# Building the convolution kernels: rounding by TensorE inside PSUM, a written-out order for the first two units, and a new layout of the staging tiles

## The chip, the cores and the metric

The program runs on one core of one Trainium2 chip. The metric is the device time of one execution in microseconds (us), taken as the median over runs. A core has five engines that work at the same time, each through its own queue of instructions in order: TensorE (PE in the profile; its weight loads are listed apart as PEld), VectorE (DVE), ScalarE (ACT), GpSimd (POOL) and SyncE (SP), which here only issues DMAs. [...]

## What is computed

Four layers on a 2048 x 640 activation: a state-space convolution, an attention with one shared key and value head, and both once more. The change lies in what both convolutions need first, the convolution kernel of each of the 640 channels d at 2048 times l:

```python
dt = exp(log_dt)[:, None]
logdA = dt * (A_re + 1j * A_im)                 # 640 x 128 states n
dB = dt * (B_re + 1j * B_im)
P = exp(logdA[:, :, None] * l[None, None, :])
K = einsum("dn,dnl,dn->dl", C, P, dB).real      # 640 x 2048
```

K is the same in both convolution layers and is computed once, at the start of the program. The kernel splits l = 32 i + s, and so writes the exponential as a product of a factor for i (64 values) and a factor for s (32 values), each a magnitude exp(...) times a cosine and a sine of an angle. The sum over the 128 states is a matmul.

## The kernel before, in words

**Tables.** `kg_tables` (L203) makes, on VectorE and ScalarE, what the angles and magnitudes are built from: for each state and channel the angle per step in whole turns (`thr`), the angle of 32 steps (`th1`), the phase of C times B (`ph`), the decay (`are`) and a log magnitude (`lw`). Each is split into three bf16 parts, staged in the tiles `hs[...]` (first in their pool, before the inputs and the scratch tiles that `t3` makes), and sent by SP into three tables that matmuls can read: `tb` (48 rows: three parts of 16 channels), `ta` and `tm` (96 rows). `send` (L222) goes through DRAM: one DMA out, then three back. `send_late` (L230) writes the lower 48 rows of `ta` or `tm` for one eighth q of the channels, three DMAs each time; q = 0 to 7 are sent one after the other, the last after all else. The order of ScalarE, VectorE and SP is written out by hand here; SP's issues of the input x (`load_x`, L611, eight DMAs of 640 KB) are not part of that order, and a planner puts them among the others.

**Units.** `_kgen` (L310) then runs 20 units u, each 2 x 16 channels. For a unit there are two angles (h = 0 from `tb`, h = 1 from `ta`) and three magnitudes (k = 0, 1, 2 from `tm`). Each is a 128 x 1024 tile in PSUM, made by two bf16 matmuls of 512 columns: the table's 16 channels by 128 states are the weights, and a constant tile `kg` is what streams.

- `phase_first(u, h)` (L366): the two matmuls of an angle into `ph`. There is one such PSUM buffer (`bufs=1`), so the next angle waits for the last reader.
- `phase(u, h)` (L374): VectorE takes the whole turns off in two passes, `magic_round` (L191; adding and subtracting 1.5 x 2^23 rounds to a whole number, kept in `r`) and a subtraction (L381), which leaves the fraction `f` in SBUF.
- `trig(u, h)` (L383): ScalarE takes Abs of `f` into `fa` (L394), Sin of `f` (L395) and Sin of a quarter turn less `fa`, the cosine (L396).
- `sizes` and `exps` (L399, L408): the matmuls of a magnitude into `pe` (two buffers) and Exp by ScalarE.
- `products(u, k)` (L416): six passes of VectorE, two for each k.
- `sums(u, ds)` (L433): the fp32 matmuls, 128 rows by 32 columns of weights and 64 columns of stream, four side by side in the array, in eight steps d. `store` (L444) copies the sum to `kst` and every fourth unit sends it to DRAM.

The loop at L469 is a software pipeline with the order of PE, ScalarE and VectorE written by hand. In iteration u stand the magnitudes and the trig of unit u, the angles of u + 1, the products of u - 1 and the sums of u - 2. Even and odd iterations differ in where Exp and Sin stand, so that ScalarE changes its table once per unit. From u = 5 to 12 VectorE also has the layer norm's statistics of one part of x (`stats`, L618). After u = 20 the tables' pool is closed and GpSimd loads the weights of the Fourier matmuls; the rest of the program, two convolutions and two attentions, follows.

## Time and profile before

| | |
|---|---|
| median of 3 runs | 3025.67 us (3024.11 to 3025.82) |
| the profiled execution | 3025.52 us, its span 3023.7 us |
| PE busy over the span | 2797.2 us (93%) |
| ScalarE busy over the span | 2427.3 us (80%) |
| VectorE busy over the span | 1402.3 us (46%) |
| tables and units (the part that the change touches) | about the first 300 us |

The page has six parts. Part 1 gives the busy time of each engine; part 2 cuts the span into 40 slices of 75.6 us, each digit being the busy share in tenths; "PEclk" is the clock that TensorE was granted. Part 4 follows back what ended last, part 5 lists the costliest groups of instructions, and part 6 the DMAs. Other views of the same execution list instructions in order of time with what each waited for, who waited for whom in a stretch, and the busy time of each engine in stretches that one chooses. A share over the whole span says little here: the attention layers, where PE and ScalarE are at 90% and over, fill three quarters of it, and the units are a stage of their own with another limit.

### The profile page before, as it was taken

To read this page: it belongs to the slowest core of one execution; us is meant where nothing else is said; L and a number is where in the kernel's file an instruction comes from. 1 tells how busy PE (TensorE), PEld (TensorE's weight loads), DVE (VectorE), ACT (ScalarE), POOL (GpSimd) and SP (SyncE) were. 2 spreads that over 40 slices of the span, in tenths; PEclk is the share of its full clock that TensorE was granted. 3 is DMA by queue.
4 is the path that set the end of the run, shared out by engine and by line. 5 is a ranking of instruction groups with operands and counts; after the bars stand their busy time and mean duration, and the time that the engine had idled before them with its cause. 6 is when DMAs were issued, how large, how long until landed. Compare 5 with 4: busy or idle time off the path is not lost. (4 is left out here: it accounts for less than half of the span.)

```text
span 3023.7 us, 52365 instructions
## 1 busy us (share of the span) xinstructions
PE 2797.2 (93%) x21696; PEld 1284.0 (42%) x21696; DVE 1402.3 (46%) x1788; ACT 2427.3 (80%) x2910; POOL 45.1 (1%) x117
## 2 busy tenths in 40 slices
PE   2776989998999999999999899798999999999998
PEld 0333979775233323333232689673233333323333
DVE  7999899942123232322323499721222223222222
ACT  5888333444999999999999532438999999999997
POOL 0001000000000000000000000000000000000000
PEclk9855999999999999999999999899999999999999
DMA  6114531133200010000100211131100101110100
GB/s 145 33 22 112 186 143 56 46 115 111 80 22 25 22 27 21 26 25 22 25 22 20 113 56 42 58 131 56 27 24 23 43 22 26 39 28 21 43 19 23
DMA packets 109104, 158.82 MB, mean 53 GB/s; under 512 B 58948, under 2 KB 65092, under 8 KB 105236
## 3 DMA queue, kind: packets, MB, share of 16 engines
q1 hardware_dynamic: 102680, 137.70, 15.7%
q0 software_dynamic: 4208, 16.67, 1.5%
q8 instruction: 175, 2.87, 0.4%
q10 hardware_dynamic: 1968, 0.98, 0.1%
q14 instruction: 73, 0.60, 0.1%
HBM read 95.22 MB, written 48.04 MB: 47 GB/s over the span
## 5 line engine op out<-in xcount | busy, mean ns | idle before, releaser
L1158 ACT ACTIVATE pt<-scb 128x1024 f32<-128x1024 f32 x1024 | 942.2, 1116 | 7.5 <-DMA qpb<-mxd 4.5
L1158 ACT ACTIVATE pt<-scd 128x1024 f32<-128x1024 f32 x1024 | 942.2, 1117 | 7.0 <-PE scd L1154 5.4
L1168 PE MATMUL pod<-pt,vt 128*32 128x512 f32 x4096 | 547.1, 606 | 4.4 <-DVE on L1185 0.2
L1168 PE MATMUL pob<-pt,vt 128*32 128x512 f32 x4096 | 547.0, 606 | 4.4 <-DVE on L1185 0.3
L1154 PE MATMUL scb<-qpb,kt 62*128 62x512 f32 x2048 | 385.9, 451 | 6.2 <-DVEq L1103 5.8
L1154 PE MATMUL scd<-qpd,kt 62*128 62x512 f32 x2048 | 385.9, 451 | 5.6 <-PEq L1103 5.3
L1154 PEld LDWEIGHTS scb<-qpb,kt 62*128 62x128 f32 x2048 | 165.9, 185 | 402.1 <-ACT pt L1158 392.6
L1154 PEld LDWEIGHTS scd<-qpd,kt 62*128 62x128 f32 x2048 | 166.0, 185 | 401.7 <-ACT pt L1158 392.4
L1216 DVE TENSOR_TENSOR x<-pyd,x 128x320 f32<-128x320 f32 x146 | 71.8, 492 | 560.8 <-PE pyd L1228 560.8
L1216 DVE TENSOR_TENSOR x<-pyb,x 128x320 f32<-128x320 f32 x146 | 71.8, 492 | 547.6 <-PE pyb L1228 547.6
L1188 DVE RECIPROCAL rc<-rc 128x512 f32<-128x512 f32 x62 | 207.9, 3354 | 2.1
L1168 PEld LDWEIGHTS pob<-pt,vt 128*32 128x32 f32 x4096 | 80.6, 108 | 178.2 <-issue 160.2
L1168 PEld LDWEIGHTS pod<-pt,vt 128*32 128x32 f32 x4096 | 80.6, 108 | 178.0 <-issue 160.0
L601 PE MATMUL za<-xna,wf 128*128 128x256 f32 x512 | 113.0, 383 | 2.5 <-ACT xna L757 2.5
L601 PE MATMUL zc<-xnc,wf 128*128 128x256 f32 x512 | 111.5, 379 | 2.7 <-ACT xnc L757 2.7
L603 ACT ACTIVATE Aa<-za 128x1024 f32<-128x1024 f32 x16 | 16.4, 1023 | 118.5 <-PE za L601 117.3
L603 ACT ACTIVATE Ac<-zc 128x1024 f32<-128x1024 f32 x16 | 16.4, 1023 | 113.7 <-PE zc L601 113.7
L1228 PE MATMUL pyd<-wo,ot 128*32 128x320 f32 x1168 | 105.3, 432 | 0.0
L1228 PE MATMUL pyb<-wo,ot 128*32 128x320 f32 x1168 | 105.3, 432 | 0.0
L601 PEld LDWEIGHTS za<-xna,wf 128*128 128x128 f32 x512 | 97.8, 192 | 16.6 <-ACT xna L757 3.3
L601 PEld LDWEIGHTS zc<-xnc,wf 128*128 128x128 f32 x512 | 96.9, 190 | 16.3 <-ACT xnc L757 3.3
L800 PE MATMUL yc<-Ac,wi 128*128 128x128 f32 x640 | 78.4, 286 | 15.8 <-DVE Ac L114 13.1
(312 smaller groups left out, 3107.2 us busy)
## 6 DMA issues: line engine op xcount, KB each, us to landing
kh<-kh SPq DMA_DIRECT2D x10, 2048.0 KB
kh<-kn SPq DMA_DIRECT2D x5, 2048.0 KB
qhd<-qh SPq DMA_DIRECT2D x40, 256.0 KB
qld<-ql SPq DMA_DIRECT2D x40, 256.0 KB
qpb<-qhd SPq DMA_DIRECT2D x256, 40.0 KB
qpd<-qhd SPq DMA_DIRECT2D x256, 40.0 KB
ot<-on SPq DMA_DIRECT2D x216, 40.0 KB
wf<-in_c_wf POOLq DMA_DIRECT2D x16, 512.0 KB, 7.9
```

Of the source, the lines that this page charges most:

```text
L601: nc.tensor.matmul(zv[:, :, c, kk], self.wf[:, t + 4 * h, j, c, kk], x, start=(n == 0), stop=(n == 3))
L603: nc.scalar.activation(A.rearrange("p (o s) d -> p o s d", o=2)[:, :, 2 * t : 2 * t + 2], z.rearrange("p (c o e) -> p o c e", c=2, o=2), A ...
L800: nc.tensor.matmul(y[:, s * DC : (s + 1) * DC], self.wi[:, t, j, c_, kk], v[:, 2 * t + c_, kk], start=(i == 0 and not whole), stop=(i == 3 ...
L1154: nc.tensor.matmul(sc[:, 512 * par : 512 * par + 512], kt[rows, 128 * t : 128 * t + 128], qps[nb, hg, pr][rows], start=True, stop=True)
L1158: nc.scalar.activation(pt, sc, AF.Exp, scale=SCALE)
L1168: nc.tensor.matmul(po[32 * j : 32 * j + 32], vt[:, t], pts[step, j // 2][:, 512 * (j % 2) : 512 * (j % 2) + 512], start=(t == 0), stop=(t ...
L1188: nc.vector.reciprocal(rc, rc)
L1216: nc.vector.tensor_tensor(xh, py, xh, ALU.add)
L1228: nc.tensor.matmul(py[j : j + m], o[:, 128 * i + j : 128 * i + j + m], w[:, 320 * half : 320 * half + 320], start=start, stop=stop)
```

## The change

It has two parts. The first is in the angles. `kg` gets two more pieces, the negatives of the two angle patterns, and a tile `unit` of one row holds 128 ones, the number M = 1.5 x 2^23 and -M in bf16. `phase_first` now issues eight matmuls for an angle in place of two. For each of the two halves: the angle as before; a one-row matmul that adds M to all 512 columns; another that adds -M; and the angle once more with its sign turned. In PSUM's fp32 that leaves the rounded angle less the angle, which is the fraction with its sign turned, and the sine's scale changes sign for it. VectorE then has one copy (`tensor_copy`) in place of two passes. For h = 1 the absolute value moves from ScalarE to VectorE (`fold`, a bitwise and). The matmuls of the second angle, `phase_first(u + 1, 1)`, move forward in the loop, ahead of `trig` and of the middle `sums`.

The second part is the opening. The first angle and its trig (`begin`) are put inside `kg_tables`, behind the phases' last part and ahead of the log magnitude; the decay's splitting and sending move forward; PE joins the engines whose order is written out. Iterations 0 and 1 are taken out of the loop and written out. Twelve scratch tiles now live in the tile of x, which is not loaded until the magnitudes of unit 0 have been computed (a one-column write into x by ScalarE orders this); `load_x` is issued by SP in that place, behind all the tables' DMAs. The staging tiles now stand behind the sixteen other scratch tiles of their pool, in the order in which they come free and with a spacer. Some tiles move to a pool of their own (`kga`) that is there from the start. The load of the identity matrix is now issued in each iteration that has sums, 20 times, in place of once.

```diff
-    kg = np.concatenate([r.reshape(96, -1) for r in (r1, r2, r3, r4)], axis=1)
+    kg = np.concatenate([r.reshape(96, -1) for r in (r1, r2, r3, r4, -r1, -r2)], axis=1)
...
+        rest("are", are, 0)
+        cast("are", are, 1)
         T(wr, wr, 0.0, 0.5, ALU.is_lt, ALU.mult)
...
         send("thr", ta)
+        rest("are", are, 1)
+        cast("are", are, 2)
+        send("are", tm)
...
         nc.vector.tensor_copy(hs["ph"][:, 2], res["ph"])
-        rest("are", are, 0)
-        cast("are", are, 1)
+        send_late(0, ta, hs["ph"])
+        begin()
         S(lw, u3, 0.5, lw, op0=ALU.mult, op1=ALU.add)
...
-        rest("are", are, 1)
-        cast("are", are, 2)
-        send("are", tm, lambda: send_late(0, ta, hs["ph"]))
...
-        kg = sp.tile([96, 2560], BF16, name="kg")
+        kg = sp.tile([96, 3584], BF16, name="kg")
+        unit = sp.tile([1, P + 2], BF16, name="unit")
+        nc.gpsimd.memset(unit[:, 0:P], 1.0)
+        nc.gpsimd.memset(unit[:, P : P + 1], MAGIC)
+        nc.gpsimd.memset(unit[:, P + 1 : P + 2], -MAGIC)
+
+        ba = ctx.enter_context(tc.tile_pool(name="kga", bufs=2, reuse_waits="tile"))
...
+            ph = PH[u, h] = kp.tile([P, 1024], F32, tag="ph", bufs=1, name=f"ph{u}{h}")
             src, col, rows = ((tb, 0, 48), (ta, 512, 96))[h]
             for par in range(2):
-                nc.tensor.matmul(pp[:, 512 * par : 512 * par + 512], grp(src, u, par, rows),
-                                 kg[0:rows, col : col + 512], start=True, stop=True)
+                o, w = ph[:, 512 * par : 512 * par + 512], grp(src, u, par, rows)
+                nc.tensor.matmul(o, w, kg[0:rows, col : col + 512], start=True, stop=False)
+                for k in range(2):
+                    nc.tensor.matmul(o, unit[:, 0:P], unit[:, P + k : P + k + 1].to_broadcast([1, 512]),
+                                     start=False, stop=False)
+                nc.tensor.matmul(o, w, kg[0:rows, 2560 + col : 3072 + col], start=False, stop=True)
...
         def phase(u, h):
...
-            r = bp.tile([P, 1024], BF16, tag="r", bufs=2, name=f"r{u}{h}")
-            self.magic_round(r, pp)
-            F[u, h] = bp.tile([P, 1024], F32, tag="f", bufs=4, name=f"f{u}{h}")
-            nc.vector.tensor_tensor(F[u, h], pp, r, ALU.subtract)
+            F[u, h] = ba.tile([P, 1024], F32, tag="f", bufs=4, name=f"f{u}{h}")
+            nc.vector.tensor_copy(F[u, h], ph)
+
+        def fold(u):
+
+            FA[u] = ba.tile([P, 1024], F32, tag="fb", bufs=1, name=f"fb{u}")
+            nc.vector.tensor_scalar(FA[u].bitcast(I32), F[u, 1].bitcast(I32), 0x7FFFFFFF, None,
+                                    ALU.bitwise_and)
...
-            fa = bp.tile([P, 1024], F32, tag="fa", bufs=1, name=f"fa{u}{h}")
-            nc.scalar.activation(fa, f, AF.Abs)
-            nc.scalar.activation(s, f.rearrange("p (a d s) -> p a d s", a=2, d=16), AF.Sin, scale=TWO_PI)
+            if h == 0:
+                fa = ba.tile([P, 1024], F32, tag="fa", bufs=1, name=f"fa{u}{h}")
+                nc.scalar.activation(fa, f, AF.Abs)
+            else:
+                fa = FA.pop(u)
+            nc.scalar.activation(s, f.rearrange("p (a d s) -> p a d s", a=2, d=16), AF.Sin, scale=-TWO_PI)
...
+        def begin():
+            phase(0, 0)
+            trig(0, 0)
...
+            homes = [self.x.rearrange("p t d -> p (t d)")[:, 640 * k : 640 * k + 640].rearrange(
+                "p (t s) -> p t s", t=5) for k in range(12)]
+            homes += [pp.tile(SH, F32, name=f"t{k}") for k in range(16)]
+
             def t3(name):
-                return pp.tile(SH, F32, name=name)
-            hs = {n: pp.tile([P, 3, 5, NST], BF16, name="h" + n)
-                  for n in ("ph", "lw", "th1", "thr", "are")}
+                return homes.pop(0)
+
+            hs = {}
+            for n in ("are", "thr", "th1", "", "ph", "lw"):
+                if n:
+                    hs[n] = pp.tile([P, 3, 5, NST], BF16, name="h" + n)
+                else:
+                    pp.tile([P, 192], F32, name="space")
...
-            for h in range(2):
-                phase(0, h)
-            for u in range(n + 3):
+            phase(0, 1)
+            phase_first(1, 0)
+            for k in range(2):
+                sizes(0, k)
+                exps(0, k)
+            phase(1, 0)
+            sizes(0, 2)
+            exps(0, 2)
+            nc.scalar.activation(self.x[:, :, 0], M1[0][:, :, 0, 0], AF.Copy)
+            self.load_x()
+            products(0, 0)
+            for k in range(2):
+                sizes(1, k)
+                exps(1, k)
+            fold(0)
+            phase(1, 1)
+            sizes(1, 2)
+            exps(1, 2)
+            trig(0, 1)
+            phase(2, 0)
+            products(0, 1)
+            trig(1, 0)
+            fold(1)
+            phase(2, 1)
+            products(0, 2)
+            trig(1, 1)
+            for u in range(2, n + 3):
...
                 if prod:
                     products(u - 1, 0)
+                if now and not odd:
+                    fold(u)
...
                 if prod:
                     products(u - 1, 1)
+                if now and odd:
+                    fold(u)
+                if nxt:
+                    phase_first(u + 1, 1)
                 if now:
                     trig(u, 0 if odd else 1)
...
                     sums(u - 2, range(7, 8))
-                if u == 0:
-                    self.load_x()
                     nc.sync.dma_start(self.ident, ins["c_id"])
```

More of the change, by code (lines that the diff above doesn't have):

```diff
@@ new lines, in _kgen, with big, swap, fl @@
+        units += [(2, r, 512 + 16 * r, 64, 64) for r in range(4)]
+        C1, S1, C2, S2, M1, M2, E1R, F, FA, PH, PE_, PK, KST = ({} for _ in range(13))
+        KST[0, 0] = ba.tile([P, 64, 32], F32, tag="kst", bufs=2, name="kst00")
+        def big(tag, u, x, bufs=2):
+            pool = ba if tag in ("c1", "s1") else bp
+            return pool.tile([P, 16, 2, x], F32, tag=tag, bufs=bufs, name=f"{tag}_{u}")
+        def swap(a):
+            return a.rearrange("p d a s -> p a d s")
+        def fl(a):
+            return a.rearrange("p d a s -> p (d a) s")
```

72 lines of the change are left out of this document (31 added, 41 removed).

## The prediction

> **What bounds the kernel now.** I read the page's slices first.
>
> ```profile
> span 3023.7 us, 52365 instructions
> PE   2776989998999999999999899798999999999998
> DVE  7999899942123232322323499721222223222222
> ACT  5888333444999999999999532438999999999997
> PEclk9855999999999999999999999899999999999999
> ```
>
> The tables and units fill the first four slices (to 300 us). There VectorE is at 9, PE at 7, and PE's granted clock falls to 5, as nowhere else. Next, the busy time of each engine in a stretch that I cut at the last product of unit 0 and of unit 17, 17 iterations, one inside it, and the stretches ahead of it:
>
> ```profile
> core 0: us, PE busy (x) PEld busy (x) DVE busy (x) ACT busy (x) POOL busy (x), PEclk, DMA share, GB/s
> 0.00:45.00 45.00, 1.03 (x2) 0.13 (x2) 37.36 (x58) 17.60 (x26) 0.54 (x8) 1.00 0.86 202
> 45.00:72.00 27.00, 12.79 (x34) 2.54 (x34) 18.95 (x17) 21.67 (x21) 0.31 (x2) 1.00 0.36 64
> 71.49:277.43 205.94, 147.39 (x2325) 68.68 (x2325) 203.88 (x195) 183.03 (x187) 7.05 (x36) 0.64 0.18 28
> 119.65:286.91 167.26, 120.54 (x1948) 57.09 (x1941) 164.26 (x159) 148.00 (x152) 8.87 (x34) 0.53 0.22 29
> ```
>
> In the cut VectorE works 203.88 of 205.94 us: it is the bound, 12.1 us a unit. PE works 147.39, 8.7 a unit, ScalarE 183.03, 10.8 a unit. The groups of that stretch and who waited for whom in it say what VectorE's time is:
>
> ```profile
> L381 DVE TENSOR_TENSOR f<-ph,r 128x1024 f32<-128x1024 f32 x34 | 41.6, 1225 | 1.8
> L191 DVE TENSOR_SCALAR r<-ph 128x1024 bf16<-128x1024 f32 x34 | 41.4, 1217 | 0.0
> L394 ACT ACTIVATE fa<-f 128x1024 f32<-128x1024 f32 x34 | 35.8, 1052 | 0.6
> L623 DVE BATCH_NORM_STATS2 st<-x 128x6 f32<-128x320 f32 x16 | 7.0, 482 | 0.0
> L624 DVE BATCH_NORM_AGGREGATE mv<-st 128x2 f32<-128x12 f32 x8 | 1.7, 209 | 0.3
> PE ph L371 <- DVE f L381: 30.4, 21, 2.8
> ```
>
> The two passes over the angles are 83 of 204 us (the statistics 8.7, so that a pass costs 195.2 / 170 = 1.15 us), and PE's largest wait is for the second of them. So a pass taken from VectorE shortens the loop, until PE or ScalarE is the bound. The question is how long PE's own queue is once it has the passes' work. Its queue, in order of time, with starts in the first column and durations in the second (the first row is VectorE's, for later):
>
> ```profile
> 25.34 0.49 DVE L269 TENSOR_SCALAR wr<-wr 128x640 f32<-128x640 f32 x1
> 53.05 1.01 PE L404 MATMUL pe<-kg,tm 48*128 48x512 bf16 x2 [6.10 <-DMA ta<-hph]
> 53.86 1.05 PE L371 MATMUL ph<-kg,tb 48*128 48x512 bf16 x2
> 54.71 1.05 PE L404 MATMUL pe<-kg,tm 48*128 48x512 bf16 x2
> 131.37 1.03 PE L404 MATMUL pe<-kg,tm 48*128 48x512 bf16 x2
> 140.13 0.60 PE L404 MATMUL pe<-kg,tm 48*128 48x512 bf16 x2
> ```
>
> From 53.86 to 54.71 two matmuls of 512 columns take 0.85 us, 0.427 each. A pair whose two overlap lasts 1.03 at this rate; the one at 140.13 lasts 0.60, at about twice the rate. So there are two rates, and the slow one rules here. (From 45 to 72 us the clock column reads 1.00, but the pairs at 53 us are slow; I go by the pairs.) Over the 49 windows of 3.41 us from 119.65 to 286.91 the clock is 0.53, which is three windows at 1.00 and the rest at 0.50. From 131.37 to 140.13 PE runs a whole odd iteration without a wait: 8.76 us. Of these, 10 bf16 matmuls are 4.27, and eight steps of sums at 0.427 are 3.41; the remaining 1.08 lie at the eight places where it goes from one shape of weights to another, 0.135 each.
>
> When does the fast rate come? The busy time by window of 3.41 us, for all of PE's work, then for the sums (L441) alone, the angles (L371) alone and the magnitudes (L404) alone:
>
> ```profile
> 133.31:136.72 3.41, 3.41 (x55) 1.40 (x54) 3.38 (x4) 1.17 (x2) 0.16 (x1) 0.50 0.02 1
> 136.72:140.13 3.41, 3.41 (x84) 2.23 (x83) 3.41 (x4) 3.29 (x4) 0.14 (x1) 0.50 0.02 5
> 140.13:143.55 3.42, 1.30 (x15) 0.32 (x12) 3.39 (x4) 3.39 (x4) 0.02 (x1) 1.00 0.00 0
> ...
> 133.31:136.72 3.41, 1.62 (x51) 1.14 (x50) 0.50 0.02 1
> 136.72:140.13 3.41, 2.51 (x80) 2.10 (x80) 0.50 0.02 5
> ...
> 136.72:140.13 3.41, 1.03 (x2) 0.13 (x2) 0.50 0.02 5
> ...
> 133.31:136.72 3.41, 2.01 (x4) 0.26 (x4) 0.50 0.02 1
> ```
>
> Both of the first two windows are busy from end to end, yet only the second is followed by 1.00. They differ in what ran. The first had 51 pieces of sums (0.0267 us each, 128 rows) and four matmuls of 0.427, two of 48 rows and two of 96; the second had 80 pieces and two matmuls of 96 rows. Weighted by rows over 128 that is 1.36 + 0.32 + 0.64 = 2.32 us (68%) against 2.13 + 0.64 = 2.77 us (81%). So what raises the clock seems to be rows at work, not a busy queue. In the third window PE had little to do, and the clock fell back.
>
> [...]
>
> **The change part by part.**
>
> *Angles on PE.* Each angle goes from 2 to 8 matmuls of 512 columns, so a unit gets 12 more: 12 x 0.427 = 5.12 us. Four of the eight have one row, and the order angle, M, -M, angle gives two changes of shape per half, eight per unit. No row shows a one-row matmul; the nearest is the change of shape above, 0.135, so 1.08 (ends: 0, and twice that). A unit's queue on PE is then 8.76 + 5.12 + 1.08 = 14.96 us at the slow rate, over VectorE's 12.1. PE becomes the bound, and no wait has to be added for that.
>
> How often will it run fast? By rows, a one-row matmul counts for nothing, so the mean falls: 3.41 us of sums, 8 x 0.427 x 48/128 = 1.28 and 6 x 0.427 x 96/128 = 1.92 of magnitudes and angles are 6.6 of 14.96 (44%). Full speed throughout is out by that. But the later sums of a unit (five steps, 2.13 us) with the 96-row magnitudes (0.64) reach 2.77 us in 3.3, which is the case of the window that did release it, if a window lies well over it. Before, 3 of about 14 units had that; with PE never idle I take 8 of 17 units, between 0 and 17. A fast window does 6.8 us of work in 3.41; its changes of shape do not shrink and VectorE has to keep up, so I take 2.7 us won: 8 x 2.7 = 21.6.
>
> PE's queue passes the first magnitudes of unit 2 and of unit 19 here:
>
> ```profile
> 73.56 1.03 PE L404 MATMUL pe<-kg,tm 48*128 48x512 bf16 x2
> 278.98 0.60 PE L404 MATMUL pe<-kg,tm 48*128 48x512 bf16 x1
> ```
>
> That is 205.42 us for 17 units. After: 17 x 14.96 - 21.6 = 232.7 us, **+27.3 us**.
>
> *VectorE and ScalarE.* VectorE has ten passes a unit and loses two, of 1.15 us, and gains `fold`, 0.8 at most and 0.7 taken (a 640-column pass of that kind took 0.49); ScalarE loses one pass of 1.05. This saves 17 x (2.3 - 0.7) = 27 us on VectorE's queue, but it ends in waiting for PE, so nothing of it counts. The statistics and `fold` are covered by the same waiting; without it they would cost 8.7 and 17 x 0.7 = 12 us.
>
> *Second angle moved forward.* It has to wait for the copy of the first (one buffer), behind 1.28 us of sums and 0.85 to 1.7 of magnitudes on PE; the copy, 1.2 us, with up to 2.3 us of products ahead of it, is mostly done by then. Behind it on PE wait sums, which nobody needs before the next store, and in even iterations one pair of magnitudes. I take zero, bounded by 17 x 0.5 either way.
>
> *Opening.* Rows of the stretch before the loop's steady state:
>
> ```profile
> 4.42 2.50 SPq L615 DMA_DIRECT2D x<-in_A_u  x4
> 19.83 0.36 SPq L224 DMA_DIRECT2D hdth<-hth  x1
> 24.46 1.29 SPq L227 DMA_DIRECT2D tb<-hdth  x3
> 36.02 0.49 DVE L291 CAST hph<-resph 128x640 bf16<-128x640 f32 x1
> 42.51 0.49 DVE L304 CAST hlw<-reslw 128x640 bf16<-128x640 f32 x1
> 45.17 1.78 SPq L232 DMA_DIRECT2D tm<-hlw  x3
> 61.03 1.22 DVE L422 TENSOR_TENSOR e1r<-m,c 128x1024 f32<-128x1024 f32 x1
> DVE r L191 <- PE ph L371: 7.9, 3, 5.5
> ```
>
> Now x is loaded among the tables (4.6 us from 19.83 to 24.46 for a small write to land), and the magnitudes of unit 0 start at 53.05. Afterwards x is out of the way. The log magnitudes, ready at 43.0 and sent at 45.17, are ready at 44.2, behind the copy of the first angle, and sent at once; the first product could stand at about 55, 6 us earlier. But PE then has in its order five angles before the magnitudes of unit 2 (unit 0's second, unit 1's and unit 2's), each 8 x 0.427 + 4 x 0.135 = 3.95 us: 19.8; six pairs of magnitudes with a change of shape, 5.9; three copies in between that the single `ph` buffer puts on the path, 1.4 each with the wake-up, 4.2; and about 1.5 for Exp to free a `pe` buffer. They start at 42: the phases are ready at 36.5 plus two decay passes of 0.75 that now come first, and sending and landing take 2 to 5 us. That gives 73.4, against 73.56. So the opening gives **0**, between -4 and +4.
>
> *Queues and memory.* SP issues x last, from about 72 us; the first statistics, in u = 5, come after 105, and eight loads of 640 KB need about 25 us at the 202 GB/s that the first 45 us had, so it is in time. The 20 loads of the identity, 64 KB each, share SP with the stores of `kst`; a store's landing matters only at the end, where none follows it. The larger `kg` is 0.2 MB more, 1 us, long before its first use. After the loop, the weights wait for the last magnitudes and so move with PE.
>
> Sum: 27.3 + 0 = +27 us against the profiled execution's 3025.52 us (0.15 under the median), **3052 us**.
>
> **The rivals.**
>
> *PE runs fast throughout* (the other side). If one-row matmuls count as activity, a queue that never idles keeps 1.00. Then 14.96 falls to about 8 and VectorE bounds again, at 8 x 1.15 + 0.7 = 9.9 a unit (ScalarE 10.8 - 1.1 = 9.7), against 11.5: 17 x 1.6 = 27 us less, and some 5 us of the opening's gain stay: 2993 us. It decides once the weighted share is over some 70 to 80% in most windows. For it speaks that PE will be dense; against it the window 133.31 to 136.72, dense and slow. [...]
>
> *PE never runs fast.* The one-row matmuls break up every window: 17 x 14.96 - 205.42 = +49, 3074 us. Against it, the later sums now stand closer together than before.
>
> *The changes of shape cost nothing for one-row matmuls, or fast windows come in nearly every unit.* 17 x 1.08 = 18 us less, or 17 windows in place of 8, 24 us less: 3028 to 3034 us, and with both the change is level with before, 3020 to 3030.
>
> **How the numbers follow.** The forecast with its nearer variations (3034 to 3068) has 0.60; never fast 0.12; cheap changes or many fast windows 0.13; level 0.05, of which I count a part as same; fast throughout 0.10. The likeliest gives 3052. The range leaves out the fast case and half of the level one, and reaches to never fast: 3024 to 3075; the likeliest one's own is 3034 to 3068. A measurement of this kernel can tell 0.2%, 6 us, from no change. Faster by more than that: 0.14; within it: 0.06; slower: 0.80.
>
> **What would show it.** Right: in the stretch between the magnitudes of units 2 and 19, PE busy for nearly all of some 233 us, VectorE at some 75% and waiting for `ph`, copies and products at the old 1.2 us, a clock of 0.5 to 0.65; pitch of units 13 to 15 us. One-row pairs would show 0.43 per matmul and a gap at each change. The first product near 55, but the magnitudes of unit 2 still near 73. The forecast is wrong if the clock in that stretch is near 1.00, with VectorE full at 10 us a unit; and too high if the gaps around the one-row matmuls are missing.

## The result and the profile after

The changed kernel takes 3056.15 us in the median (3051.23 to 3056.44, four runs), the kernel before, run beside it, 3024.89 us (3023.11 to 3025.82): a ratio of 1.0101, with a 95% interval of 1.0088 to 1.0113. It is slower, by 1%. The profiled execution of the changed kernel took 3051.23 us (span 3049.4), against 3025.52 (span 3023.7): 25.7 us more in the spans. It is the shortest of its four runs; the other three lie at 3056, which matters below.

The slices of the page after:

```profile
span 3049.4 us, 52826 instructions
PE   3999889998999999999999899798999999999999
DVE  6877899953122322232232499822222222222223
PEclk9755899999999999999999999899999999999999
```

Set beside those of before, PE is at 9 in the second to fourth slices (it was at 7, 7 and 6), VectorE has come down to 7 and 8, and the low digits of the clock last one slice longer. After the fifth slice the two pages are alike. So the difference lies where the change was made.

To split it I need a mark that is the same work in both kernels. I take the start of the first pass of a unit's last products (`c<-c,m`): unit 0's ends "the opening", and from there to unit 17's are 17 iterations, "the loop". The busy time of the engines in the loop, before and after (in each row the time, then PE, PEld, VectorE, ScalarE, POOL, and PE's clock):

```profile
70.35:276.30 205.95, 148.38 (x2326) 68.81 (x2327) 203.89 (x195) 183.05 (x186) 7.05 (x36) 0.64 0.18 27
```

```profile
77.23:302.18 224.95, 219.23 (x2514) 79.10 (x2517) 174.44 (x178) 163.27 (x167) 13.96 (x36) 0.61 0.25 43
94.29:302.18 207.89, 202.30 (x2335) 73.37 (x2328) 159.64 (x164) 153.76 (x157) 13.10 (x33) 0.57 0.19 29
```

The opening ends at 77.23 in place of 70.35 (+6.9 us), the loop takes 224.95 in place of 205.95 (+19.0 us), and what follows is 0.2 us shorter: together the 25.7 us. In the loop the bound has changed hands. VectorE was busy for 99% of it, now for 78%; PE was busy for 72%, now for 97%. The second row after leaves out the start, where the clock column reads 1.00 although the pairs of matmuls at 82.31 and 89.69 us still last 1.03 us: without it the clock is 0.57. What the engines wait for in the loop confirms it; VectorE's largest wait is for the last matmul of an angle:

```profile
DVE f L368 <- PE ph L360: 51.5, 23, 3.3
ACT m L443 <- PE pe L435: 28.4, 8, 4.8
```

Now PE's own queue. The first rows below are an angle that runs at the slow rate in the opening, the last three are the first magnitudes of three units that follow each other in the loop (start, duration):

```profile
47.01 0.58 PE L356 MATMUL ph<-kg,ta 96*128 96x512 bf16 x1 [13.88 <-DMA tm<-hlw]
47.52 1.03 PE L358 MATMUL ph<-unit 1*128 1x512 bf16 x2
48.48 0.61 PE L360 MATMUL ph<-kg,ta 96*128 96x512 bf16 x1
48.88 0.63 PE L356 MATMUL ph<-kg,ta 96*128 96x512 bf16 x1
49.45 1.03 PE L358 MATMUL ph<-unit 1*128 1x512 bf16 x2
...
207.95 1.03 PE L435 MATMUL pe<-kg,tm 48*128 48x512 bf16 x2
222.71 1.03 PE L435 MATMUL pe<-kg,tm 48*128 48x512 bf16 x2
237.20 0.81 PE L435 MATMUL pe<-kg,tm 48*128 48x512 bf16 x2
```

From one pair of one-row matmuls to the next are 1.93 us (47.52 to 49.45): four matmuls of 0.427 are 1.71, and 0.22 are left for two changes of shape. Units that run at the slow rate throughout stand 14.76 and 14.49 us apart, 14.62 in the mean. Without matmuls and sums (22 x 0.427 and 3.41) 1.8 us remain for 16 changes of shape, 0.11 each.

Last, four of the 3.41 us windows in which the clock is granted (in the loops of before and after each stretch at one rate lasts a multiple of 3.413 us), with all of PE's work, the sums alone (L472) and the one-row matmuls alone (L358):

```profile
224.00:227.41 3.41, 3.41 (x8) 0.48 (x7) 2.19 (x2) 0.81 (x1) 0.15 (x1) 0.50 0.01 2
227.41:230.82 3.41, 3.41 (x53) 1.66 (x53) 3.18 (x3) 1.02 (x1) 0.00 (x0) 0.50 0.03 7
234.24:237.65 3.41, 3.41 (x84) 2.40 (x84) 2.64 (x3) 3.40 (x5) 0.00 (x0) 0.50 0.00 0
237.65:241.06 3.41, 3.41 (x44) 1.10 (x42) 3.41 (x4) 3.41 (x5) 0.14 (x1) 1.00 0.23 27
...
227.41:230.82 3.41, 1.73 (x48) 1.25 (x48) 0.50 0.03 7
234.24:237.65 3.41, 2.36 (x80) 2.12 (x80) 0.50 0.00 0
237.65:241.06 3.41, 0.65 (x32) 0.49 (x32) 1.00 0.23 27
...
237.65:241.06 3.41, 1.20 (x4) 0.22 (x4) 1.00 0.23 27
```

All four windows are full. The first, with eight matmuls of 512 columns, and the second, with 48 pieces of sums, are not followed by the full rate; the third, with 80 pieces of 128 rows, is. The fourth has the full rate and loses it again: a third of it went to one-row matmuls. Ten such windows of full rate stand in the loop, and all ten last a single window.

### The profile page after: what moved, and what is told of

Its sections match the earlier page's. It is cut to its first block, busy times and chain, and to the rows that moved or that the text cites. A ratio compares the mean times of both kernels' runs of the same rounds, so it can differ in the third digit from the quotient of the medians.

```text
span 3049.4 us, 52826 instructions
## 1 busy us (share of the span) xinstructions
PE 2889.1 (95%) x21936; PEld 1299.5 (43%) x21936; DVE 1366.7 (45%) x1768; ACT 2405.8 (79%) x2891; POOL 53.0 (2%) x120
## 5 line engine op out<-in xcount | busy, mean ns | idle before, releaser
L1228 PEld LDWEIGHTS pob<-pt,vt 128*32 128x32 f32 x4096 | 80.6, 108 | 177.6 <-issue 159.7
L663 ACT ACTIVATE Aa<-za 128x1024 f32<-128x1024 f32 x16 | 16.4, 1024 | 118.4 <-PE za L661 117.1
L663 ACT ACTIVATE Ac<-zc 128x1024 f32<-128x1024 f32 x16 | 16.4, 1024 | 113.6 <-PE zc L661 112.7
L661 PEld LDWEIGHTS zc<-xnc,wf 128*128 128x128 f32 x512 | 97.8, 192 | 16.3 <-ACT xnc L817 3.1
L860 PE MATMUL yc<-Ac,wi 128*128 128x128 f32 x640 | 78.7, 286 | 14.6 <-DVE Ac L114 11.9
```

The source lines that it names most:

```text
L661: nc.tensor.matmul(zv[:, :, c, kk], self.wf[:, t + 4 * h, j, c, kk], x, start=(n == 0), stop=(n == 3))
L663: nc.scalar.activation(A.rearrange("p (o s) d -> p o s d", o=2)[:, :, 2 * t : 2 * t + 2], z.rearrange("p (c o e) -> p o c e", c=2, o=2), A ...
L860: nc.tensor.matmul(y[:, s * DC : (s + 1) * DC], self.wi[:, t, j, c_, kk], v[:, 2 * t + c_, kk], start=(i == 0 and not whole), stop=(i == 3 ...
L1228: nc.tensor.matmul(po[32 * j : 32 * j + 32], vt[:, t], pts[step, j // 2][:, 512 * (j % 2) : 512 * (j % 2) + 512], start=(t == 0), stop=(t ...
```

## The experiments

Two things were to be told apart: how much of the time is the clock's, the one-row matmuls' or the changes of shape's, and what the opening does. The theory is the prediction's: the loop is PE's queue, at a clock that counts rows at work, and the opening gives nothing. The rivals stand with each run. The table gives all of it; "opening" and "loop" are as defined above, from the profiled execution of each kernel. Each run was timed beside the kernel before (3024.4 to 3025.0 us).

| kernel | median us | ratio, 95% interval | opening ends | loop | PE / VectorE busy in the loop |
|---|---|---|---|---|---|
| before | 3024.89 | | 70.35 | 205.95 | 148.4 / 203.9 |
| changed | 3056.15 | 1.0088 to 1.0113 | 77.23 | 224.95 | 219.2 / 174.4 |
| opening alone | 3031.37 | 1.0010 to 1.0028 | 68.75 | 213.42 | 146.8 / 204.2 |
| turns alone | 3054.46 | 1.0082 to 1.0113 | 75.48 | 230.25 | 224.3 / 174.5 |
| 128 rows | 3007.48 | 0.9934 to 0.9961 | 76.02 | 185.67 | 151.7 / 173.3 |
| matching rows | 3006.59 | 0.9926 to 0.9953 | 74.81 | 184.16 | 153.6 / 173.4 |
| crossed rows | 3032.77 | 1.0019 to 1.0040 | 77.27 | 202.24 | 177.6 / 174.3 |
| 32 rows | 3054.86 | 1.0079 to 1.0108 | 77.56 | 227.65 | 221.8 / 174.4 |
| one row, grouped | 3039.80 | 1.0040 to 1.0066 | 76.13 | 216.60 | 208.1 / 174.4 |
| 64/128 rows, queue order | 3002.49 | 0.9919 to 0.9945 | 67.95 | 188.63 | 148.7 / 173.5 |
| old opening, 64/128 rows | 3004.10 | 0.9920 to 0.9945 | 69.86 | 188.10 | 150.6 / 173.6 |
| opening alone, tile moved | 3025.41 | 0.9993 to 1.0011 | 68.76 | 207.75 | 149.2 / 204.2 |
| 64/128, order, tile moved | 3000.04 | 0.9906 to 0.9933 | 69.39 | 184.98 | 151.9 / 173.4 |
| changed, opening mended | 3050.29 | 1.0072 to 1.0099 | 72.03 | 228.97 | 224.2 / 174.6 |

### The two parts apart

The opening alone is the changed kernel with the two old matmuls and VectorE's two passes for an angle, Abs by ScalarE and the second angle back in its old place in the loop; the turns alone are the kernel before with `phase_first`, `phase`, `fold` and `trig` of the change and the second angle moved forward.

```diff
 # opening alone
-                nc.tensor.matmul(o, w, kg[0:rows, col : col + 512], start=True, stop=False)
...
+                nc.tensor.matmul(ph[:, 512 * par : 512 * par + 512], grp(src, u, par, rows),
+                                 kg[0:rows, col : col + 512], start=True, stop=True)
...
-            nc.vector.tensor_copy(F[u, h], ph)
+            self.magic_round(r, ph)
+            nc.vector.tensor_tensor(F[u, h], ph, r, ALU.subtract)
```

> The changed kernel with its first part alone: the opening as changed, the angles as before (two matmuls, two passes of VectorE, Abs by ScalarE). Theory (PE's longer queue took all of the loss and hid a gain of the opening): the first product stands near 55 us instead of 61, the magnitudes of unit 2 at 67 to 71 instead of 73.56, and the time is 3 to 7 us under before, 3018 to 3022. Rival (the opening itself costs the 2.4 us by which the changed kernel is late at unit 2): 3026 to 3030.

```diff
 # turns alone, on the kernel before
+                for k in range(2):
+                    nc.tensor.matmul(o, unit[:, 0:P], unit[:, P + k : P + k + 1].to_broadcast([1, 512]),
+                                     start=False, stop=False)
+                nc.tensor.matmul(o, w, kg[0:rows, 2560 + col : 3072 + col], start=False, stop=True)
...
-            self.magic_round(r, pp)
-            nc.vector.tensor_tensor(F[u, h], pp, r, ALU.subtract)
+            nc.vector.tensor_copy(F[u, h], ph)
```

> The kernel before with the second part alone: eight matmuls an angle, one copy by VectorE, the absolute value of the second angle by VectorE, the second angle moved forward; opening, pools and loads as before. Theory: PE bounds the loop as in the changed kernel, 226 to 236 us between the magnitudes of units 2 and 19 against 205.4, and since PE is also busier in the opening the time is 25 to 38 us over before, 3050 to 3063. Rival (a good part of the loss is in the opening's part): under 3045.

The turns alone gave 3054.46 us, as expected, and account for nearly all of the loss; their loop, 230.25 us, is PE's (97% busy). The opening alone missed: 3031.37 us, 1 us over the rival's range, and 6 us slower than before where the theory had a gain. Its trace shows why (ScalarE, then VectorE):

```profile
77.37 1.15 ACT L381 ACTIVATE c<-fa,halfpi 128x1024 f32<-128x1024 f32 x1 [7.98 <-DMA tm<-hlw]
...
88.63 1.23 DVE L442 TENSOR_TENSOR e1r<-m,c 128x1024 f32<-128x1024 f32 x1 [5.87 <-PE pk L461]
```

ScalarE stands for 7.98 us at unit 1's second cosine until the transfers out of the staging tile `hlw` have been read: the buffer that this cosine goes to lies on that tile. VectorE is then idle for 5.87 us ahead of 88.63, behind the sums that come after. Whether this is the loss was left to a run of its own, below.

### Rows: what the clock counts

M and -M were added by weights with more rows, all of them zero but the first, so that the sum is the same.

```diff
-        unit = sp.tile([1, P + 2], BF16, name="unit")
-        nc.gpsimd.memset(unit[:, 0:P], 1.0)
+        unit = sp.tile([128, P + 2], BF16, name="unit")
+        nc.gpsimd.memset(unit[:, 0:P], 0.0)
+        nc.gpsimd.memset(unit[0:1, 0:P], 1.0)
...
-                    nc.tensor.matmul(o, unit[:, 0:P], unit[:, P + k : P + k + 1].to_broadcast([1, 512]),
+                    nc.tensor.matmul(o, unit[0:128, 0:P],
+                                     unit[0:128, P + k : P + k + 1].to_broadcast([128, 512]),
```

> The changed kernel with 128 rows in place of one in the matmuls that add M and -M: 127 of the rows have weights of zero, so the sums are the same, and their number, columns and durations at a given rate are unchanged. Theory (the granted clock follows the rows at work): the weighted share rises from 6.6 to 10.0 of 14.96 us a unit (67%), the clock is at 1.00 for most of the loop, VectorE bounds it at about 10 to 11 us a unit, and the time is 2995 to 3012, under before. Rival (the clock follows something else, or rows of zero weights do not count): the queue is as long as in the changed kernel, less what one kind of change of shape saves, 3045 to 3058.

The second has 48 rows for the first angle and 96 for the second, like the angles themselves.

```diff
-                    nc.tensor.matmul(o, unit[:, 0:P], unit[:, P + k : P + k + 1].to_broadcast([1, 512]),
+                    nc.tensor.matmul(o, unit[0:rows, 0:P],
+                                     unit[0:rows, P + k : P + k + 1].to_broadcast([rows, 512]),
```

> The changed kernel with as many rows in the added matmuls as in the angle beside them (48 and 96, all but one with zero weights), so that no change of shape is left inside an angle. Theory: the eight changes are gone, 8 x 0.135 x 17 = 18 us at the slow rate, and the weighted share is 8.5 of 13.9 us (61%), enough for more windows at 1.00; both together 2997 to 3025. Rival (the clock does not follow the rows): the changes of shape alone, 3034 to 3042; and if they cost nothing, 3050 to 3058.

Both met the theory: 3007.48 and 3006.59 us, 49 us under the changed kernel, and under the kernel before. The number of matmuls and of columns is the same, and so is what VectorE does. The loop of the matching rows:

```profile
74.81:258.97 184.16, 153.55 (x2514) 74.49 (x2517) 173.41 (x179) 161.38 (x168) 14.02 (x36) 0.85 0.31 54
```

PE's busy time falls from 219.2 to 153.6 us, the clock rises from 0.61 to 0.85 (behind the start, where the column reads 1.00, from 0.57 to 0.84 between 110 and 250 us), and VectorE is the bound again (94%). But with matching rows all eight changes of shape of a unit go, and with 128 rows the second angle's four (that the two kernels are equal fits with neither being bound by PE any more), so these runs don't tell rows from shape. The next two do: one gives rows and keeps every change (128 rows with the angle of 48, 64 with the angle of 96), the other takes half of the changes away and gives no row. What counts as a change of shape is seen in the starts of the matmuls that follow each other at the slow rate: from 96 rows to 128 and from 48 to 64 it is 0.40 to 0.43 us, as within one shape; from 1 to 48 or 96, from 48 to 128 and from 64 to 96, and back, it is some 0.56. The matmul behind the changed one then follows after 0.40, so that two take 0.96 in place of 0.85, and 0.11 is the price.

```diff
 # crossed rows
+                    n = (128, 64)[h]
+                    nc.tensor.matmul(o, unit[0:n, 0:P], unit[0:n, P + k : P + k + 1].to_broadcast([n, 512]),
 # one row, grouped: both halves of each kind, in place of a half at a time
+            for o, w in zip(os, ws):
+                nc.tensor.matmul(o, w, kg[0:rows, col : col + 512], start=True, stop=False)
+            for k in range(2):
+                for o in os:
+                    nc.tensor.matmul(o, unit[:, 0:P], unit[:, P + k : P + k + 1].to_broadcast([1, 512]),
+                                     start=False, stop=False)
+            for o, w in zip(os, ws):
+                nc.tensor.matmul(o, w, kg[0:rows, 2560 + col : 3072 + col], start=False, stop=True)
```

> The changed kernel with the matmuls of M and -M over 128 rows for the first angle (whose own matmuls have 48) and over 64 rows for the second (whose own have 96), all rows but one with zero weights: rows are added and every change of shape stays, eight in a unit. Theory (the granted clock alone is what the earlier two row experiments gained): by the milestone rows of the 128-row run the gain lay in the clock, so 3003 to 3015 us, as near 3007 as that run's 3007.5; the first stage's clock as there. Rival (a good part of the 49 us gained there came from the changes of shape that went, 17 units x 8 x 0.11 to 0.135 us = 15 to 18 us): 3020 to 3035 us.

> The changed kernel with the one-row matmuls kept, but the order within an angle changed: both halves' first addition, both halves' M, both halves' -M, both halves' second addition. Four changes of shape in a unit go, no row is added and no matmul. Theory (PE bounds the loop and a change of shape costs it 0.11 to 0.135 us; the clock is not moved by it): 17 x 4 x 0.11 to 0.135 = 7.5 to 9.2 us less, 3047 to 3049 us, range 3042 to 3052. Rival (the changes of shape cost nothing, the gaps are only the starting of a matmul): 3054 to 3058 us.

My theory of the clock alone fell. The crossed rows gave 3032.77 us, inside the rival's range, and the grouping 3039.80, below mine. So of the 49 us, rows alone bring 23 (3056 to 3033), and the rest came where the changes of shape went too. It isn't for want of rows: crossed rows add more of them (128 and 64) than matching rows (48 and 96), and are 26 us slower. Their loops in the traces, crossed rows first, then grouped:

```profile
77.27:279.51 202.24, 177.56 (x2514) 69.41 (x2530) 174.29 (x178) 161.35 (x166) 13.99 (x36) 0.80 0.27 47
```

```profile
76.13:292.73 216.60, 208.07 (x2514) 83.13 (x2517) 174.40 (x179) 163.39 (x167) 13.99 (x36) 0.62 0.27 46
```

With crossed rows the loop is 16.6 us longer than with 128 rows, which keep four of the eight changes (17 x 4 x 0.11 = 7.5), and 18.1 longer than with matching rows, which keep none (17 x 8 x 0.11 = 15). So the price of the changes is not all of it, and the terms don't simply add, since VectorE bounds the two others; in the traces 31 of some 59 windows have the full rate with crossed rows, 35 of 54 with matching rows. The medians lie still further apart, 25 to 26 us. The eight runs of the crossed kernel reach from 3023.97 (the profiled one) to 3039.89, and their granted clock over the whole span falls by and large along with that, from 0.972 to 0.965; why it differs from run to run stays open. The grouped loop is 8.4 us shorter than the changed kernel's, against 17 x 4 x 0.11 = 7.5; but it also has eleven windows of full rate in place of ten, so this alone would not prove the price. The slow units stand 14.32 and 14.04 us apart in its trace (first magnitudes at 178.92, 193.24 and 207.28), 0.44 less than before grouping: four changes of 0.11. The whole is 11.9 us shorter by the profiled executions and 16.4 by the medians; the rest of it stands in the opening (1.1), behind unit 17 (2.3) and in the spread of the changed kernel's own runs (5).

Last, 32 rows, to ask what counts as a row:

```diff
-                    nc.tensor.matmul(o, unit[:, 0:P], unit[:, P + k : P + k + 1].to_broadcast([1, 512]),
+                    nc.tensor.matmul(o, unit[0:32, 0:P],
+                                     unit[0:32, P + k : P + k + 1].to_broadcast([32, 512]),
```

> The changed kernel with the matmuls of M and -M over 32 rows, 31 of them with zero weights, the shape change left as it is with one row. [...] Theory (the rows that are streamed count, so 32 rows raise the row-weighted share of a unit a little, from some 43 to 50%): a few more windows at full rate, 3040 to 3053 us. Rival (rows below a quarter of the array count as one quarter in either case, or are too few to release more windows): 3054 to 3058 us, as the changed kernel.

3054.86 us, the rival's range: in the median nothing is gained (the five runs reach from 3044.20 to 3056.76). Yet it doesn't show that a quarter of the rows is counted as none. I weighted each matmul's time in each window of the loop by its rows over 128, from the trace, with 0.427 us for 512 columns and 0.0267 for a piece of the sums, and half of that at the full rate. In the 32-row kernel nine slow windows are followed by the full rate: one has a share of 0.67, the others 0.71 or more. Those that are not followed by it reach up to 0.67. In the changed kernel the ten that are followed by it have 0.64 to 0.81, and of the others none has over 0.66; in the kernel before the four have 0.71 to 0.81, and of the others none has over 0.66. The added rows fall where the share was low, and do not lift it there to that of the windows that were followed by the full rate.

The same weighing over the loops of all fourteen traces tells how far this goes. (A trace's first stretch, before its clock has an event, is counted as slow.) Of 584 windows at the slow rate, the share that parts them best, 0.67, leaves 6 on the wrong side; of 274 windows at the full rate, 0.35 leaves 1, the clock being lost below it. By busy time alone, without rows, the best dividing shares leave 90 and 53 wrong. With 32 rows as the least that a matmul counts for, as the rival of this run has it, they leave 8 and 11. So rows are what fits best, though not exactly: two windows of the matching rows, with hardly anything but matmuls of 96 rows (0.75 and 0.76), are among the six and were not followed by the full rate. Nor did the full rate come only behind windows with sums. In the old opening with 64 and 128 rows, a run of the next section, a window with seven matmuls of 512 columns on record and not a piece of sums was followed by it:

```profile
253.13:256.54 3.41, 2.99 (x7) 0.99 (x7) 2.41 (x3) 3.38 (x5) 0.15 (x1) 0.50 0.77 95
256.54:259.95 3.41, 3.01 (x93) 1.59 (x92) 3.13 (x3) 3.41 (x5) 0.00 (x0) 1.00 0.79 101
```

### The opening

Three read-backs of the magnitude table stand in SP's queue behind a write that they wait for, and the first late send of the phase table behind those. In the next kernel, with 64 and 128 rows, they were put behind that send:

```diff
+            nc.sync.dma_start(HD[n], hs[n].rearrange("p k t s -> p k (t s)"))
...
-        send("are", tm)
+        send_out("are")
...
         send_late(0, ta, hs["ph"])
+        send("are", tm)
         begin()
```

> The changed kernel with M and -M over 64 rows for the first angle and 128 for the second (zero weights but in one row), and in the opening the three read-backs of the magnitude table moved behind the first late send of the phase table in SP's queue, so that this send does not wait for the staged write's landing. Theory: the rows give 3007 as before; the first late send is issued some 3 us earlier (38.7 instead of 41.7 us into the span), TensorE's second angle begins some 3 us earlier, and unit 0's products end 2 to 3 us earlier, which a loop that VectorE bounds keeps: 3002 to 3006 us. Rival (the magnitude table, now later in the queue, is what the first exponentials then wait for, or the loop catches up by itself): 3006 to 3010 us.

3002.49 us, as the theory had it, but the parts came out larger and one against the other. SP's issues in the changed kernel, in order of time:

```profile
35.20 0.43 SPq L224 DMA_DIRECT2D hdare<-hare  x1
40.40 1.25 SPq L226 DMA_DIRECT2D tm<-hdare  x3
41.70 1.83 SPq L231 DMA_DIRECT2D ta<-hph  x3
```

Its wait ahead of the second of these (total, times, longest):

```profile
SPq L226 <- DMA hdare<-hare: 4.7, 1, 4.7
```

SP's first late send, PE's second angle, and ScalarE's cosine of unit 1, in the kernel with the new order:

```profile
36.12 3.28 SPq L238 DMA_DIRECT2D ta<-hph  x3
...
41.79 0.59 PE L365 MATMUL ph<-kg,ta 96*128 96x512 bf16 x1 [8.88 <-DMA ta<-hph]
...
74.85 1.15 ACT L402 ACTIVATE c<-fb,halfpi 128x1024 f32<-128x1024 f32 x1 [8.62 <-DMA tm<-hlw]
```

The send is through SP's queue at 39.40 in place of 43.53, and the second angle starts 5.2 us earlier (41.79 for 47.01), not 3. (The row at 47.01 names `tm<-hlw`, the transfer next in the queue, as what ended the wait; the matmul itself reads `ta`.) With that the opening ends 6.9 us earlier than with matching rows (67.95 for 74.81). But unit 1's cosine comes now before the staging tile is free, waits 8.62 us, and the loop gives back 4.5 us.

The old opening with the same rows (the turns alone, with 64 and 128 rows of weights) asks whether the new one is worth anything there:

```diff
+                    n = (64, 128)[h]
+                    nc.tensor.matmul(o, unit[0:n, 0:P], unit[0:n, P + k : P + k + 1].to_broadcast([n, 512]),
```

> The kernel before with the turns taken off by TensorE alone (the opening and the staging tiles as before), M and -M over 64 rows for the first angle and 128 for the second. Theory (what the opening loses is its own order and lies ahead of the loop whatever the rows; the changed opening alone took 6.3 us more than the kernel before, of which the wait on the staging tiles, 6 to 8 us, is hidden at 0.6 us in the row experiments): 3003 to 3012 us, within 4 us of the 3006.6 of the matching rows. Rival (the late start of unit 0's products, 6.9 us in the changed kernel, is the changed opening's and goes with it): 2998 to 3002 us.

3004.10 us (interval of the ratio nearly the same as above): the theory's range. The opening ends at 69.86. Between the two openings nothing can be told.

Then the staging tile was moved 8.4 KB on, away from unit 1's cosine, once with the old angles and once on the kernel with 64 and 128 rows:

```diff
             for n in ("are", "thr", "th1", "", "ph", "lw"):
+                if n == "lw":
+                    pp.tile(SH, F32, tag="frac", bufs=2, name="frac")
+                    pp.tile([P, 832], F32, name="space2")
                 if n:
```

> The opening alone, with the angles reduced by VectorE as before, and the staging tile of the log magnitudes 8.4 KB further on in its pool, so that it lies under unit 2's second-factor sine tile and no longer under unit 1's cosine tile. Nothing else is moved. Theory (the opening alone lost what unit 1's cosine waited for the transfers out of this tile, 8.0 us on ScalarE and 5.9 us of VectorE's idle time behind it): 3031.4 less 5.9 to 8.0 = 3023 to 3026 us. Rival (that wait only stands where another would, VectorE or TensorE being late there anyway): 3029 to 3032 us.

> The kernel with 64 and 128 rows and the read-backs moved behind the first late send (3002.5 us), with the same staging tile moved in the same way. There ScalarE waited 8.6 us for it, and VectorE 3.5 us behind that. Theory: 3.5 to 6 us less, TensorE being what is late next: 2996 to 3000 us. Rival (the loop, bounded by VectorE at nine tenths, gives nothing more): 3001 to 3004 us.

The opening alone fell from 3031.37 to 3025.41 us, as expected, and unit 1's cosine no longer waits (unit 2's sine, on the tile's new place, waits 2.4 us). So the collision was its loss. What is left is no gain either: 1.0002 of the kernel before (0.9993 to 1.0011). Its opening ends 1.6 us earlier, and its loop is 1.8 us longer, with two windows of full rate in place of four; but the profiled run, 3027.44 us, is the longest of its eleven, so that the ratio says more than the trace.

On the other kernel the same edit gave 3000.04 us, on the edge of the expected range; the wait is gone, and PE's magnitudes are what ScalarE then waits for. Against 3002.49 the difference is too small for the intervals to tell. It has the lowest median of all, 0.8% under the kernel before (0.9906 to 0.9933). Its loop:

```profile
69.39:254.37 184.98, 151.87 (x2514) 73.48 (x2517) 173.35 (x178) 161.22 (x167) 13.99 (x36) 0.86 0.32 57
```

The last run puts both mends, the two diffs above, into the changed kernel itself, one-row matmuls and all:

> The changed kernel with its one-row matmuls and only its opening mended: the read-backs of the magnitude table behind the first late send of the phase table in SP's queue, and the staging tile of the log magnitudes 8.4 KB further on. It asks whether the opening's 6.9 us lie in the time. Theory (they do, since TensorE is busy from the first angle to the end of the loop and what starts earlier ends earlier): the second angle begins some 5 us earlier, as the same edit showed with more rows (41.8 for 47.0 us), and the whole is 4 to 8 us less, 3045 to 3052 us. Rival (the loop or what follows it takes the gain back): 3054 to 3058 us.

3050.29 us, 5.9 less than the changed kernel by the medians and in the theory's range, although the intervals of the two ratios overlap a little (1.0072 to 1.0099, 1.0088 to 1.0113). Since both mends are in it, it doesn't say what each is worth. The opening ends 5.2 us earlier. In the trace the loop is 4.0 us longer, 228.97 us, with eight windows of full rate in place of ten; but the changed kernel's trace is its shortest run, 5 us under its median, so the medians and not the two traces should be compared.

## Why the prediction was right, and where it was not

The time was foretold as 3052 us and came as 3056 (3051 in the trace). The mechanism of the loop was right; of the two terms, by the marks used above, one was 8 us too large and the other 7 us too small, and so their sum was nearer than its parts. Part of that is one wrong mark, which enters both terms and cancels; the rest is luck.

*PE becomes the bound.* Right. PE is busy for 97% of the loop, VectorE for 78%, and the passes that VectorE saved end in waiting for `ph` (51.5 us).

*The queue of 14.96 us at the slow rate.* Nearly: 14.62. The one-row matmuls take 0.427 us like any other. The mis-sized term is the change of shape, 0.11 us in place of 0.135, which the grouped kernel confirms within a unit (0.44 us for four). At the full rate the price is the same, as the prediction took it to be: in the changed kernel's window from 90.88 us, 0.31 us from start to start at the change and 0.23 behind it, 0.11 more than two matmuls at half of 0.427.

*Eight fast windows at 2.7 us.* There were ten. 17 units of 14.62 are 248.5 us; less the 224.95 measured, ten windows brought 23.6 us, 2.4 each, against 21.6 foretold. With the same figures the other kernels with one-row or 32-row weights should come to 229.6 us for eight windows and 227.3 for nine. The turns alone (eight) have 230.25, the mended kernel (eight) 228.97, 32 rows (nine) 227.65. So in these four traces the loop's length is the slow queue less 2.4 us for each window. Why the changed kernel's other three runs are 5 us longer stays open: they have no trace, and their granted clock over the whole span, 0.954 for 0.953, doesn't tell of fewer windows.

*+27.3 us in the loop.* It is +19.0 by the marks used above, 224.95 us where 232.7 were forecast. The shorter pitch is 5.8 us of the difference, the windows are 2, and half a microsecond is the other mark.

*Rows count, not a busy queue.* Right, and it decides the result. The rival "fast throughout" was 2993 us and needed one-row matmuls to count as activity. They didn't: with PE busy for 97% of the loop the clock was 0.57 behind the start; given rows of their neighbours' shape, nearly the same program takes 3007 us. Nor did a full window bring the full rate by itself: in the changed kernel full windows with a weighted share up to 0.66 were not followed by it. What I had wrong was to hold the changes of shape for a small matter beside it: with rows added, the kernel that keeps all eight is still 25 to 26 us slower than the two others by the medians.

*The opening gives 0.* Wrong: +6.9 us. Two steps failed. One is the mark: "73.56" is not the first magnitude pair of unit 2 in the trace of before but its second. The first is here, with the first pairs of units 2 and 19 in the changed kernel below it, unit 2's 9.1 us later:

```profile
66.87 1.03 PE L404 MATMUL pe<-kg,tm 48*128 48x512 bf16 x2
...
75.98 1.03 PE L435 MATMUL pe<-kg,tm 48*128 48x512 bf16 x2
304.35 1.03 PE L435 MATMUL pe<-kg,tm 48*128 48x512 bf16 x2
```

So the sum of 73.4 was held against a time 6.7 us too late, and a loss looked like nothing. The same slip stands in the loop's term: 205.42 us lead from unit 2's second pair to unit 19's first, from first to first it is 212.11. With the right mark the prediction's own sums make +20.6 for the loop and +6.5 for the opening; the same marks measure +16.3 (228.37) and +9.1. So the slip moved 6.7 us from one term to the other, and against the sum it does nothing; that the loop's remaining 4.3 too much and the opening's 2.6 too little lie on opposite sides is the luck. The other step is "They start at 42". PE's second angle started at 47.01, because SP issues in order and the three read-backs, moved ahead of the late send, waited 4.7 us for the staged write to land. With both mends it started at 41.8, where the sum had it, and the changed kernel came out 5.9 us shorter by the medians. From its start to 75.98 the opening took 29.0 us, against 31.4 worked out: that part held. The turns alone, with the old opening, end theirs at 75.48, 5.1 us later than before: the longer angles cost that much, and the new order with its late start did not win it back. The first product came at 59.26, not near 55, behind magnitudes that PE began at 56.13, after unit 0's second angle and unit 1's first.

*Queues and memory.* The prediction had not looked at which buffers the staging tiles now lie under. In the changed kernel the wait is covered, since PE is later still. In the opening alone it costs 6 us, and it comes back as soon as the opening is made faster. The statistics never showed up as a wait, and for the weights GpSimd stood 0.5 us once. The second angle moved forward was not tried apart.

*The rivals' sums.* Cheap changes and fast windows in every unit together would be 18 and 24 us under 3052, which makes 3010 us and not 3020 to 3030; the argument doesn't rest on it.

## What to carry to other kernels

Work that is moved to an engine with idle time is paid at the clock that this engine will be granted (0.57 of the full one here, behind the start of the loop), with all gaps that the new instructions bring (0.11 us each here): write out its queue for one unit, and weigh matmuls by their rows before counting on the full rate. Where a matmul with few rows stands between larger ones, try zero weights that bring it to its neighbours' shape; here they cost no time of their own (0.427 us either way) and took 49 us off. When a step is moved ahead in a queue, look at what it will wait for and who stands behind it (SP's wait of 4.7 us held up the send behind it here), and choose a mark for both traces that is the same instruction in each.

## What the runs showed of the hardware

A matmul with one row took as long as one with 128, 0.427 us for 512 columns at the slow rate. In nearly all windows of the loops the clock went with the rows: weighted by rows over 128, windows from a share of about 0.67 on were followed by the full rate (6 of 584 on the wrong side), and it was lost again below about 0.35 (1 of 274), while with matching rows five windows in a row kept it (218.6 to 235.6 us). The shares hang on how the time is weighed, and both figures are fitted to the windows of these fourteen traces and shown for no others. A change of shape cost 0.11 us at either rate, and row counts of 48 and 64, or of 96 and 128, made no change (0.40 to 0.43 us from start to start at the slow rate, as within one shape). Whether a change also keeps windows from the full rate beyond the time that it takes is not shown; the kernel with crossed rows lost more than that price. In the changed kernel the clock column reads 1.00 until its first event, at 90.88 us, although the matmuls before it run at the slow rate, 1.03 us a pair (0.57 in place of 0.61 for the loop). And in the changed kernel a write of 0.5 MB to DRAM held SP up for 4.7 us before it could be read back; two writes of the same size earlier in the opening did so for 2.1 us each.
